# Attention and two expert layers in one kernel: weight blocks loaded and converted later, more warm-up matmuls

## The chip, the cores and the metric

The kernel runs on one core of one Trainium2 chip. The metric is device time in microseconds (us); lower is better. Five engines work side by side, each through its own list of instructions in order: TensorE (PE, matmuls and transposes into PSUM), VectorE (DVE), ScalarE (ACT), GpSimd (POOL) and SyncE (SP), which here does nothing but issue DMA transfers. They wait for each other by semaphores.

## What is computed

All inputs are float32 except `w_in` and `w_out`, which are float64: they reach the kernel as 8-byte words and are turned into float32 on the chip. This turning is what the text calls a conversion.

```
for b in range(12):                      # blocks of 64 positions, per batch (2) and head (8)
    intra = (q_b @ k_b.T * Dmask) @ v_b
    inter = (q_b * lam_pow) @ kv_state
    out[b] = intra + inter
    kv_state = lam**64 * kv_state + (k_b * rev_pow).T @ v_b
...
x = out as 1536 tokens x 512
h = relu(x @ w_in); x = (h * h) @ w_out           # 512 -> 2048 -> 512
...
top-1 routing of x over 8 experts, each 512 -> 1024 -> 512, scaled by two gates
```

## The kernel before, in words

There are three stages. Attention works in 12 units (a batch and a chunk of 128 positions; batches alternate). The dense layer works in steps s (a chunk of 512 tokens and one of 16 slices of `w_in`), and the experts come last. The order of instructions on every engine is the order in which the code is written; nothing reorders them.

One turn u of the attention loop (line 436) writes, in this order: `emit_tmp(u)` on POOL; `wload(WL[u])`, DMA issues for so many weight blocks; `load_qk(u + 4)` and `load_v(u + 3)`, more DMA issues on the same SP queue; `emit_T(u + 2)`, transposes of q and k on PE, five copies on ACT and two products (qd, kd) on POOL; `emit_S(u + 1)`, scores on PE and their mask on DVE (sm); `flush()`, the second half of the conversions that were begun in the turn before; `emit_O(u)`, the output matmuls on PE (L307 with the state, L312 with v), then xTh on ACT and xTl on DVE; `emit_St(u)`, the state's matmuls (L338) and its update on DVE; and `wconv(WA[u], pO)`, the first half of WA[u] conversions. T(u), S(u), O(u), St(u) and sm(u) stand for these pieces below, whatever turn they are written in; q, k and v of unit u are q(u), k(u), v(u).

Weight blocks are numbered i0, i1, ... in the order of loading: even ones are slices of `w_in`, odd ones of `w_out`. A block is 512 KB and lands in one of 4 staging buffers (`st`); the buffer comes free when its conversion is done. q, k and v of one unit are 256 KB each. A conversion (`conv_w`, line 120) has four instructions: ACT scales the high words (L133), DVE shifts the low words (L134), DVE joins the two (L137, `shifted`), and DVE sets the sign (L141, `signed`). Between L133 and L137 the value lies in a PSUM bank, the tile `cv` of pool `pO` with tag "po", of which there is one; with `pool=None` it lies in the destination itself (`wiF`, `woF`) and the joined words in the staging buffer. The last unit's output, `po` of O(11), uses the same single "po" bank.

The weight slices are split once more into a high and a low part for the matmuls (`split_in`: wih on ACT, wil on DVE; `split_out`: woh and wol). `mm1(s)` is 12 matmuls of 512 columns (L367); in each group of three, the first two use wih and the third wil. `mm1(0)` stands in turn 11 ahead of O(11), `mm1(1)` behind the loop, `mm1(2)` in the dense loop behind them. `split_in(0)` and `split_in(1)` stand in turn 10, `split_in(2)` after the activation of step 0. `warm_pe(n)` writes n 128x128 matmuls of the identity into an unused bank.

Of the kernel before, what the change touches and what calls it, by code (L numbers as in the profile page):

```python
# [24 lines left out]
def attn_moe_kernel(ctx, tc, q, k, v, lam, w_in, w_out, w_gate, w_ogate, w1, w2, out):  # L25
# [84 lines left out]
    def load_w(i):  # L110
        f = i // 2
        t = st_p.tile([P, PC], I64, tag="st", name="st")
        if i % 2 == 0:
            nc.sync.dma_start(out=t.rearrange("p (k f) -> p k f", k=KC),
                              in_=w_in[:, f * P:(f + 1) * P].rearrange("(k p) f -> p k f", p=P))
        else:
            nc.sync.dma_start(out=t, in_=w_out[f * P:(f + 1) * P, :])
        staged[i] = t

    def conv_w(i, mid=None):  # L120
        f = i // 2
        t = staged.pop(i)
        if i % 2 == 0:
            dst = wiF[:, :, f * P:(f + 1) * P]
            sh = lambda a: a.rearrange("p (k f) -> p k f", k=KC)
        else:
            dst = woF[:, f, :]
            sh = lambda a: a
        w = t.bitcast(U32).rearrange("p (n w) -> p n w", w=2)
        lo, hi = w[:, :, 0], w[:, :, 1]  # L130
        big = dst if mid is None else sh(mid)
        out_ = sh(lo) if mid is None else big.bitcast(U32)
        nc.scalar.activation(out=big, in_=sh(hi).bitcast(F32), func=AF.Copy, scale=2.0 ** -112)  # L133
        nc.vector.tensor_scalar(out=lo, in0=lo, scalar1=29, scalar2=None, op0=ALU.logical_shift_right)  # L134

        def shifted():
            nc.vector.scalar_tensor_tensor(out=out_, in0=big.bitcast(U32), scalar=3, in1=sh(lo),  # L137
                                           op0=ALU.logical_shift_left, op1=ALU.bitwise_or)

        def signed():  # L140
            nc.vector.scalar_tensor_tensor(out=dst.bitcast(U32), in0=sh(hi), scalar=0x80000000, in1=out_,  # L141
                                           op0=ALU.bitwise_and, op1=ALU.bitwise_or)
        return shifted, signed
# [9 lines left out]
    pO = sa.enter_context(tc.tile_pool(name="pO", bufs=1, space=PSUM))  # L153
# [18 lines left out]
    NU = len(units)  # L172
    qkv = {}

    def load_qk(u):
        b, c = units[u]
        cs = slice(c * P, (c + 1) * P)
        tq = ldqk.tile([P, HP, P], F32, tag="q", name="q")
        for a in range(2):

            nc.sync.dma_start(out=tq[a * D:(a + 1) * D], in_=q[b, a::2, cs, :].rearrange("h (s r) d -> s h (r d)", r=2))
        tk = ldqk.tile([P, H, D], F32, tag="k", name="k")
        nc.sync.dma_start(out=tk, in_=k[b, :, cs, :].rearrange("h s d -> s h d"))
        qkv[u] = [tq, tk]

    def load_v(u):
        b, c = units[u]
        tv = ldv.tile([P, H, D], F32, tag="v", name="v")
        nc.sync.dma_start(out=tv, in_=v[b, :, c * P:(c + 1) * P, :].rearrange("h s d -> s h d"))
        qkv[u].append(tv)  # L190
# [14 lines left out]
    def warm_pe(n):  # L205
        for i in range(n):
            nc.tensor.matmul(out=pw_[:, i % HP, :], lhsT=ident, rhs=ident, start=True, stop=True)
# [43 lines left out]
    def emit_T(u):  # L251
        qt, kt = qkv[u][0:2]
        b, c = units[u]
        psT = pT.tile([P, 2, 2, HP, D], F32, tag="psT", name="psT")
        for hp in range(HP):
            for a in range(2):
                sl = slice(a * D, (a + 1) * D)
                nc.tensor.transpose(psT[:, a, 0, hp, :], qt[sl, hp, :], ident[sl, sl])
        for hp in range(HP):
            for a in range(2):  # L260
                sl = slice(a * D, (a + 1) * D)
                nc.tensor.transpose(psT[:, a, 1, hp, :], kt[sl, 2 * hp:2 * hp + 2, :].rearrange("p h d -> p (h d)"),
                                    ident[sl, sl])
        qT, kT = qT2[u % 2], kT2[u % 2]
        kv = kT.rearrange("p h (g t) -> p g h t", g=2)
        for a in range(2):
            for r in range(2):
                nc.scalar.copy(out=qT[a * D:(a + 1) * D, :, r::2], in_=psT[r * D:(r + 1) * D, a, 0])  # L268
        nc.scalar.copy(out=kv, in_=psT[:, :, 1])
        kTs[u] = kT  # L270
        if c > 0:
            qd = wa.tile([P, HP, P], F32, tag="qd", name="qd")
            nc.gpsimd.tensor_tensor(out=qd, in0=qT, in1=lrow, op=ALU.mult)  # L273
            qds[u] = qd
        if c < NCH - 1:
            kd = wa.tile([P, H, D], F32, tag="kd", name="kd")
            nc.gpsimd.tensor_tensor(out=kd, in0=kt, in1=mask[:, :, P - 1:P].to_broadcast([P, H, D]), op=ALU.mult)  # L277
            kds[u] = kd

    def emit_S(u):  # L280
        qT, kT = qT2[u % 2], kTs.pop(u)
        sm = wa.tile([P, H, P], F32, tag="sm", name="sm")
        ps = [pS.tile([P, HP, P], F32, tag=f"ps{a}", name="ps") for a in range(2)]
        for hp in range(HP):
            for a in range(2):

                sl = slice(a * D, (a + 1) * D)
                nc.tensor.matmul(out=ps[a][:, hp, :], lhsT=kT[sl, hp, :], rhs=qT[sl, hp, :], start=True, stop=True)
        for a in range(2):
            nc.vector.tensor_mul(sm[:, a::2, :], ps[a], mask[:, a::2, :])  # L290
        sms[u] = sm
# [27 lines left out]
    def emit_tmp(u):  # L319
        b, c = units[u]  # L320
        if c in (0, NCH - 1):
            return
        tmps[u] = tmp = wa.tile([P, HP, D], F32, tag="tmp", name="tmp")
        for a in range(2):
            sl = slice(a * D, (a + 1) * D)
            nc.gpsimd.tensor_tensor(out=tmp[sl], in0=state[b][sl, :, a * D:(a + 1) * D], in1=lblk[sl], op=ALU.mult)
# [32 lines left out]
    def mm1(s):  # L359
        ch, f = divmod(s, NF)  # L360
        wih, wil = wis.pop(s)
        ps = pm.tile([P, NTC], F32, tag="ps", name="ps")
        tk = slice(ch * NTC, (ch + 1) * NTC)
        n = 0
        for kk in range(KC):
            for w_, x_ in ((wih, xTh), (wih, xTl), (wil, xTh)):
                nc.tensor.matmul(out=ps, lhsT=w_[:, kk, :], rhs=x_[:, kk, tk], start=n == 0, stop=n == 3 * KC - 1)  # L367
                n += 1
        hps[s] = ps
# [18 lines left out]
    def split_in(s, eng=nc.vector):  # L388
        f = s % NF
        wis[s] = split(wiF[:, :, f * P:(f + 1) * P], "wi", [P, KC, P], eng)  # L390
# [8 lines left out]
    def wload(n):  # L399
        for _ in range(n):  # L400
            if wl[0] < NPC:
                load_w(wl[0])
                wl[0] += 1

    def wconv(n, pool=None):
        m = min(n, NPC - wc[0])
        wc[0] += m
        return [conv_w(wc[0] - m + i, pool and pool.tile([P, PC], F32, tag="po", name="cv")) for i in range(m)]

    rest_ = []  # L410

    def flush():
        for step in range(2):
            for r_ in rest_:
                r_[step]()
        rest_.clear()

    WA = (0,0,0,0,1,1,0,1,1,1,1,1)
    WL = (0,0,1,1,0,1,1,1,1,1,1,1)
    load_qk(2)  # L420
    load_v(0)
    nc.scalar.dma_start(out=tab.rearrange("(p n) w -> p (n w)", p=P), in_=tabi)
# [2 lines left out]
    powers(32, P + 1)  # L425
    for t in state:
        nc.vector.memset(t, 0.0)
    warm_pe(3)
    load_qk(3)
    load_v(1)  # L430
    load_v(2)
# [4 lines left out]
    for u in range(NU):  # L436

        emit_tmp(u)
        wload(WL[u])
        if u + 4 < NU:  # L440
            load_qk(u + 4)
        if u + 3 < NU:
            load_v(u + 3)
        if u + 2 < NU:
            emit_T(u + 2)
        if u == NU - 3:

            sqk.close()
            sp[0] = sab.enter_context(tc.tile_pool(name="sp", bufs=2, side="right", reuse_waits="tile"))
        if u == NU - 2:  # L450
            split_in(0)
        if u < NU - 1:
            emit_S(u + 1)
        if u == NU - 2:
            split_in(1)
        flush()
        if u == NU - 1:
            mm1(0)
        emit_O(u)
        emit_St(u)  # L460
        rest_ += wconv(WA[u], pO)
    flush()
    mm1(1)
    wload(2)
    sa.close()


# [662 lines left out]
```

## Time and profile before

| what | value |
|---|---|
| median of 3 runs | 562.34 us (560.24 to 564.80) |
| profiled execution, its time | 559.54 us |
| profiled execution, its span | 557.7 us |
| PE busy | 537.9 us (96% of the span) |
| DVE busy | 355.5 us (64%) |
| ACT busy | 303.9 us (54%) |
| POOL busy | 151.0 us (27%) |
| granted TensorE clock, mean | 0.994 of full |

Attention fills about the first 58 us of the span, the dense layer the time from there on. The busy shares are means over all stages: which engine or transfer ends the wait is read from the stretch that is asked about. In the timelines a row is a group of like instructions: its start, its length, the engine, the line, what it writes and reads, how many, and in brackets how long the engine had sat idle before it and what ended that.

### The profile page before, as it was taken

The numbers are of one execution on the slowest core, as the hardware profiler recorded it, in microseconds if no ns is written. First come the engines' busy times: TensorE is split into PE (matmuls) and PEld (weight loads), VectorE is DVE, ScalarE is ACT, GpSimd is POOL, SyncE is SP. The second block draws the span as 40 slices with busy tenths as digits, with TensorE's granted clock in tenths as the row PEclk, the third lists the DMA queues.
The fourth block names the chain that finished last, engine by engine and source line by source line (L and its number), as shares of the span: only waits on it lengthen the run. The fifth ranks groups of instructions, "written<-read, shape, count | busy, mean of one in ns | idle before, by whom it ended". The sixth has DMA issues, their size and how long they took to land.

```text
span 557.7 us, 9780 instructions
## 1 busy us (share of the span) xinstructions
PE 537.9 (96%) x3601; PEld 459.3 (82%) x3601; DVE 355.5 (64%) x714; ACT 303.9 (54%) x577; POOL 151.0 (27%) x166
## 2 busy tenths in 40 slices
PE   7998799999999999999999999999999999999994
PEld 6987678877878888887888888889898889888983
DVE  3787788989555674547676446948264949875610
ACT  4766477676643443445445434447264857884610
POOL 8886000000021232422124241450313142240101
PEclk8999999999999999999999999999999999999998
DMA  8999346466500010000000003999738567830000
GB/s 200 235 257 263 117 121 210 164 219 227 193 1 1 20 38 21 1 0 1 19 20 19 20 0 119 368 225 366 216 113 292 194 215 254 285 135 20 9 22 25
DMA packets 75045, 72.88 MB, mean 131 GB/s; under 512 B 30181, under 2 KB 61029, under 8 KB 74976
## 3 DMA queue, kind: packets, MB, share of 16 engines
q1 hardware_dynamic: 70624, 62.96, 36.3%
q0 software_dynamic: 4064, 8.91, 5.1%
q8 instruction: 43, 0.70, 0.5%
q14 instruction: 26, 0.21, 0.1%
q10 hardware_dynamic: 288, 0.10, 0.1%
HBM read 65.84 MB, written 9.29 MB: 135 GB/s over the span
## 4 chain that ended last, share of the span: by engine, by line
PE 71%; issue 12%; DMA 5%; POOL 4%; DVE 3%; ACT 2%; SPq 1%; POOLq 0%; ACTq 0%; DVEq 0%
PE acc L492 23%; PE ps L367 22%; PE ph L931 11%; PE ea L953 10%; DMA k<-in_k_dram 2%; DMA out_dram<-y,sidx 2%; POOL out_dram L963 1%; PE px L705 1%; POOL kd L277 1%; ACT ca L268 1%; PE pt L910 1%; DMA st<-in_moe_w_in_dram 1%; POOL qd L273 1%; PE pl L523 1%; PE po L307 1%
## 5 line engine op out<-in xcount | busy, mean ns | idle before, releaser
L355 POOL TENSOR_TENSOR wol<-woF,woh 128x512 fp32r<-128x512 f32 x32 | 41.4, 1293 | 224.6 <-ACT woh L354 224.6
L385 DVE TENSOR_TENSOR gl<-g,gh 128x512 fp32r<-128x512 f32 x48 | 52.7, 1097 | 65.3 <-ACT gh L384 65.3
L931 PE MATMUL ph<-xh,xTh 128*128 128x192 f32 (+2 forms) x256 | 76.9, 301 | 0.7 <-DVE xl L916 0.5
L367 PE MATMUL ps<-xTh,wih 128*128 128x512 f32 x192 | 76.6, 399 | 0.8 <-ACT wih L354 0.8
L492 PE MATMUL acc<-gl,woh 128*128 128x512 f32 x192 | 75.5, 393 | 0.0
L492 PE MATMUL acc<-gh,woh 128*128 128x512 f32 x192 | 75.0, 390 | 0.5 <-DVE x1T L504 0.5
L367 PE MATMUL ps<-xTh,wil 128*128 128x512 f32 x192 | 74.9, 390 | 0.0
L367 PE MATMUL ps<-xTl,wih 128*128 128x512 f32 x192 | 74.8, 390 | 0.0
L492 PE MATMUL acc<-gh,wol 128*128 128x512 f32 x192 | 74.8, 390 | 0.0
L931 PE MATMUL ph<-xh,xTl 128*128 128x192 f32 (+2 forms) x256 | 74.7, 292 | 0.0
L931 PE MATMUL ph<-xl,xTh 128*128 128x192 f32 (+2 forms) x256 | 74.3, 292 | 0.0
L946 DVE SCALAR_TENSOR_TENSOR hl<-ph,hh 128x384 fp32r<-128x384 f32 (+1 forms) x64 | 34.3, 536 | 61.8 <-ACT hh L945 61.7
L354 ACT CAST woh<-woF 128x512 fp32r<-128x512 f32 x48 | 29.5, 615 | 56.5 <-PE acc L492 56.5
L931 PEld LDWEIGHTS ph<-xh,xTh 128*128 128x128 f32 x256 | 48.6, 190 | 6.9 <-DVE hl L946 4.9
L945 ACT ACTIVATE hh<-ph 128x384 fp32r<-128x384 f32 (+1 forms) x64 | 30.9, 483 | 37.0 <-PE ph L931 33.8
L931 PEld LDWEIGHTS ph<-xl,xTh 128*128 128x128 f32 x256 | 48.6, 190 | 0.8
L931 PEld LDWEIGHTS ph<-xh,xTl 128*128 128x128 f32 x256 | 48.8, 190 | 0.2 <-DVE xTl L806 0.2
L374 ACT ACTIVATE r<-ps 128x512 f32<-128x512 f32 x48 | 28.5, 595 | 35.5 <-PE ps L367 35.5
L890 POOL DMA_INDIRECT xg<-x1d,gidx x21 | 23.9, 1140 | 83.9 <-PE pt L910 62.2
L963 POOL DMA_INDIRECT out_dram<-y,sidx x23 | 23.7, 1030 | 76.9 <-ACT y L962 74.4
L806 DVE TENSOR_TENSOR xTl<-w1r,xTh 128x512 fp32r<-128x512 f32 x64 | 43.7, 686 | 0.1
L492 PEld LDWEIGHTS acc<-gl,woh 128*128 128x128 f32 x192 | 36.1, 188 | 9.1 <-DVE gl L385 1.8
(192 smaller groups left out, 1150.2 us busy)
## 6 DMA issues: line engine op xcount, KB each, us to landing
w1r<-in_moe_w_dram SPq DMA_DIRECT2D x32, 512.0 KB, 6.8
w2r<-in_moe_w_dram SPq DMA_DIRECT2D x32, 512.0 KB, 6.6
st<-in_moe_w_in_dram SPq DMA_DIRECT2D x16, 512.0 KB, 4.3
st<-in_moe_w_out_dram SPq DMA_DIRECT2D x16, 512.0 KB, 3.6
q<-in_q_dram SPq DMA_DIRECT2D x24, 128.0 KB, 3.9
k<-in_k_dram SPq DMA_DIRECT2D x12, 256.0 KB, 4.1
v<-in_v_dram SPq DMA_DIRECT2D x12, 256.0 KB, 4.5
x1d<-xr SPq DMA_DIRECT2D x12, 256.0 KB, 2.0
```

The lines of the kernel that those rows point to most:

```text
L354: nc.scalar.copy(out=hi, in_=src)
L355: eng.tensor_tensor(out=lo, in0=src, in1=hi.bitcast(F32), op=ALU.subtract)
L367: nc.tensor.matmul(out=ps, lhsT=w_[:, kk, :], rhs=x_[:, kk, tk], start=n == 0, stop=n == 3 * KC - 1)
L374: nc.scalar.activation(out=r, in_=ps, func=AF.Relu)
L385: nc.vector.tensor_tensor(out=gl, in0=g, in1=gh.bitcast(F32), op=ALU.subtract)
L492: nc.tensor.matmul(out=acc[ch][cb], lhsT=w_[:, cs], rhs=x_, start=f == 0 and i == 0, stop=f == NF - 1 and i == 2)
L806: eng.tensor_tensor(out=lo, in0=src, in1=hi.bitcast(F32), op=ALU.subtract)
L931: nc.tensor.matmul(out=ps[:, 0:N], lhsT=w_[:, kk, :], rhs=x_[:, kk, 0:N], start=n == 0, stop=n == 3 * KC - 1)
L945: nc.scalar.activation(out=hh[:, f, ts_], in_=ps[:, ts_], func=AF.Relu)
L946: nc.vector.scalar_tensor_tensor(out=hl[:, f, ts_], in0=ps[:, ts_], scalar=0.0, in1=hh[:, f, ts_].bitcast(F32), op0=ALU.max, op1=ALU.subtract)
L953: nc.tensor.matmul(out=ea[j], lhsT=h_[:, f, js], rhs=w_, start=f == 0 and i == 0, stop=f == NF2 - 1 and i == 2)
L963: nc.gpsimd.indirect_dma_start(out=outs[j][:, :], out_offset=bass.IndirectOffsetOnAxis(ap=sidx[:, j, e:e + 1], axis=0), in_=ys[j], in_offs ...
```

## The change

Five lines are edited. The table WL says how many weight blocks a turn loads. Turns 0 to 7 each load q and k of a unit, the last ones in turn 7. Up to and with turn 7, five blocks are loaded in the kernel before (turns 2, 3, 5, 6, 7) and three in the changed one (turns 3, 4, 6); by the end of the loop they are 9 and 8, and the `wload` behind the loop makes it 11 in both. The table WA says how many conversions a turn begins: the same 7, begun in turns 4, 5, 7, 8, 9, 10, 11 before and 5, 6, 8, 9, 10 (two), 11 now. In turns 10 and 11 they no longer use the PSUM bank. The second `warm_pe`, between T(0) and T(1), has 8 calls where it had 3.

```
-    WA = (0,0,0,0,1,1,0,1,1,1,1,1)
-    WL = (0,0,1,1,0,1,1,1,1,1,1,1)
+    WA = (0,0,0,0,0,1,1,0,1,1,2,1)
+    WL = (0,0,0,1,1,0,1,0,1,2,1,1)
...
-    warm_pe(3)
+    warm_pe(8)
...
-        rest_ += wconv(WA[u], pO)
+        rest_ += wconv(WA[u], pO if u < NU - 2 else None)
     flush()
     mm1(1)
-    wload(2)
+    wload(3)
```

SP's queue around the last loads of q and k, before. `q_748` and `k_751` are q(10) and k(10), `q_831` and `k_834` are q(11) and k(11); `st_746`, `st_829`, `st_913` and `st_992` are the blocks i3, i4, i5 and i6.

```order
L117 DMA st_746<-in_moe_w_out_dram 128x512
L181 DMA q_748<-in_q_dram 64x4x128 x2
L183 DMA k_751<-in_k_dram 128x8x64
L189 DMA v_753<-in_v_dram 128x8x64
L114 DMA st_829<-in_moe_w_in_dram 128x4x128
L181 DMA q_831<-in_q_dram 64x4x128 x2
L183 DMA k_834<-in_k_dram 128x8x64
L189 DMA v_836<-in_v_dram 128x8x64
L117 DMA st_913<-in_moe_w_out_dram 128x512
L189 DMA v_915<-in_v_dram 128x8x64
L114 DMA st_992<-in_moe_w_in_dram 128x4x128
```

The blocks i3 and i4 stand ahead of q(11). The same place in the changed kernel, where `q_746`, `k_749` are unit 10, `q_830`, `k_833` unit 11, and `st_744`, `st_911`, `st_988`, `st_990` the blocks i2, i3, i4, i5:

```order
L114 DMA st_744<-in_moe_w_in_dram 128x4x128
L181 DMA q_746<-in_q_dram 64x4x128 x2
L183 DMA k_749<-in_k_dram 128x8x64
L189 DMA v_751<-in_v_dram 128x8x64
L181 DMA q_830<-in_q_dram 64x4x128 x2
L183 DMA k_833<-in_k_dram 128x8x64
L189 DMA v_835<-in_v_dram 128x8x64
L117 DMA st_911<-in_moe_w_out_dram 128x512
L189 DMA v_913<-in_v_dram 128x8x64
L114 DMA st_988<-in_moe_w_in_dram 128x4x128
L117 DMA st_990<-in_moe_w_out_dram 128x512
```

The blocks i3 and i4 have moved behind q(11) and k(11), and i5 follows i4 at once.

DVE's list from the split of wil(1) in turn 10 to the split of wil(2), before; the conversions are those of i4, i5 and i6:

```order
L137 SCALAR_TENSOR_TENSOR cv<-cv,st 128x512
L141 SCALAR_TENSOR_TENSOR wiF<-st,cv 128x4x128
L316 TENSOR_TENSOR xTl<-po,xTh 128x4x128
L134 TENSOR_SCALAR st<-st 128x512
L137 SCALAR_TENSOR_TENSOR cv<-cv,st 128x512
L141 SCALAR_TENSOR_TENSOR woF<-st,cv 128x512
L316 TENSOR_TENSOR xTl<-po,xTh 128x4x128
L134 TENSOR_SCALAR st<-st 128x512
L137 SCALAR_TENSOR_TENSOR cv<-cv,st 128x512
L141 SCALAR_TENSOR_TENSOR wiF<-st,cv 128x4x128
L355 TENSOR_TENSOR wil<-wiF,wih 128x512
```

The first L316 is that of unit 10, the second that of unit 11. The same stretch in the changed kernel, from the last instruction of i3's conversion on (its L137 stands ahead of it), with those of i4 and i5 together and then i6:

```order
L141 SCALAR_TENSOR_TENSOR woF<-st,cv 128x512
L316 TENSOR_TENSOR xTl<-po,xTh 128x4x128
L134 TENSOR_SCALAR st<-st 128x512 x2
L137 SCALAR_TENSOR_TENSOR st<-wiF,st 128x512
L137 SCALAR_TENSOR_TENSOR st<-woF,st 128x512
L141 SCALAR_TENSOR_TENSOR wiF<-st 128x4x128
L141 SCALAR_TENSOR_TENSOR woF<-st 128x512
L316 TENSOR_TENSOR xTl<-po,xTh 128x4x128
L134 TENSOR_SCALAR st<-st 128x512
L137 SCALAR_TENSOR_TENSOR st<-wiF,st 128x512
L141 SCALAR_TENSOR_TENSOR wiF<-st 128x4x128
L355 TENSOR_TENSOR wil<-wiF,wih 128x512
```

There are four conversions in it now, not three, and from L134 x2 on none of them names the PSUM tile `cv`.

## Rows read from the trace of the kernel before

**Rows 1.** The page's chain of waits: shares of the span by engine.
```profile
PE 71%; issue 12%; DMA 5%; POOL 4%; DVE 3%; ACT 2%; SPq 1%; POOLq 0%; ACTq 0%; DVEq 0%
```

**Rows 2.** Stretches: length, busy us (count) by engine, PEclk, DMA share, GB/s.
```profile
40.00:50.00 10.00, 9.39 (x187) 8.63 (x181) 8.03 (x15) 6.80 (x15) 8.53 (x9) 1.00 1.02 266
...
60.00:70.00 10.00, 6.54 (x52) 4.92 (x51) 6.32 (x12) 3.70 (x7) 0.00 (x0) 1.00 0.33 105
```

**Rows 3.** Timeline of PE: start us, us, engine, line, what, [idle before].
```profile
36.31 0.47 PE L258 MATMUL psT<-ident,q 64*128 64x64 f32 x8
37.15 0.46 PE L262 MATMUL psT<-ident,k 64*128 64x64 f32 x8 [0.37 <-DMA k<-in_k_dram]
...
40.85 0.46 PE L258 MATMUL psT<-ident,q 64*128 64x64 f32 x8
...
44.23 0.63 PE L338 MATMUL pt<-v,kd 128*64 128x64 f32 x16
...
51.73 0.46 PE L262 MATMUL psT<-ident,k 64*128 64x64 f32 x8
...
58.42 0.50 PE L367 MATMUL ps<-xTh,wih 128*128 128x512 f32 x1
```

**Rows 4.** Timeline of PE: O(11), and the first and third matmul of mm1(2).
```profile
64.09 1.09 PE L307 MATMUL po<-qd,ca 128*64 128x128 f32 x16 [2.61 <-DVE woF L141]
...
69.88 0.50 PE L367 MATMUL ps<-xTh,wih 128*128 128x512 f32 x1 [0.84 <-ACT wih L354]
...
70.61 0.50 PE L367 MATMUL ps<-xTh,wil 128*128 128x512 f32 x1
```

**Rows 5.** Timeline of DVE, from sm(10) to wil(2).
```profile
53.17 1.29 DVE L290 TENSOR_TENSOR sm<-ps,ca 128x512 f32<-128x512 f32 x2 [1.08 <-PE ps L288]
...
57.55 0.68 DVE L355 TENSOR_TENSOR wil<-wiF,wih 128x512 fp32r<-128x512 f32 x1
...
60.79 0.69 DVE L141 SCALAR_TENSOR_TENSOR wiF<-st,cv 128x512 uint32<-128x512 uint32 x1
...
66.71 0.69 DVE L316 TENSOR_TENSOR xTl<-po,xTh 128x512 fp32r<-128x512 f32 x1 [2.77 <-ACT xTh L315]
...
68.11 0.70 DVE L137 SCALAR_TENSOR_TENSOR cv<-cv,st 128x512 uint32<-128x512 uint32 x1 [0.38 <-ACT cv L133]
...
69.86 0.69 DVE L355 TENSOR_TENSOR wil<-wiF,wih 128x512 fp32r<-128x512 f32 x1 [0.33 <-ACT wih L354]
```

**Rows 6.** The chain of waits in order of time: start us, us, what; k(10) and i6.
```profile
41.35 4.79 DMA k<-in_k_dram
...
51.78 4.29 DMA st<-in_moe_w_in_dram
```

**Rows 7.** Stretches up to the landing of k(7), k(8), k(11): GB/s stand last.
```profile
0.00:32.57 32.57, 27.91 (x448) 25.73 (x448) 18.49 (x38) 19.88 (x43) 27.33 (x57) 0.95 0.89 222
0.00:37.15 37.15, 32.07 (x528) 29.57 (x529) 22.37 (x44) 23.06 (x50) 30.61 (x60) 0.95 0.90 226
...
0.00:51.73 51.73, 44.93 (x768) 41.28 (x769) 34.77 (x68) 32.68 (x70) 42.69 (x73) 0.97 0.92 233
```

**Rows 8.** Groups on DVE by form, 0 to 200 us: conversions without and with PSUM.
```profile
L137 DVE SCALAR_TENSOR_TENSOR st<-wiF,st 128x512 uint32<-128x512 uint32 x12 | 8.2, 686 | 0.0
...
L137 DVE SCALAR_TENSOR_TENSOR cv<-cv,st 128x512 uint32<-128x512 uint32 x7 | 4.9, 693 | 0.5 <-ACT cv L133 0.4
```

**Rows 9.** Timeline of POOL: qd(10).
```profile
48.80 1.28 POOL L273 TENSOR_TENSOR qd<-ca,ca 128x512 f32<-128x512 f32 x1 [1.21 <-PE po L307]
```

**Rows 10.** Timeline of PE, early: second warm-up, T(1).
```profile
6.75 0.94 PE L207 MATMUL pw__157<-ident 128*128 128x128 f32 x6
9.14 0.69 PE L258 MATMUL psT<-ident,q 64*128 64x64 f32 x8 [1.46 <-ACT ca L269]
```

**Rows 11.** Stretches around two waits of PE; PEclk is third from the end.
```profile
9.00:12.00 3.00, 2.86 (x32) 2.64 (x32) 0.00 (x0) 1.69 (x6) 2.96 (x5) 0.50 0.94 226
...
61.00:64.00 3.00, 0.47 (x3) 0.04 (x1) 2.80 (x5) 0.64 (x1) 0.00 (x0) 1.00 0.39 118
```

## The prediction

> **What bounds the kernel now.** The page's chain of waits comes first: 71% of the span is PE work, so time is saved where PE waits [rows 1]. The view by stretches shows where that is: between 60 and 70 us PE works 6.54 of 10 us, at the seam between attention and the dense layer [rows 2]. Over the whole span PE is busy for 96%, so I take what follows the seam as fixed: the kernel ends earlier by what the third matmul of mm1(2) starts earlier, now at 70.61 [rows 4]. (It is the third because the first two need only wih.)
>
> Two waits set that moment. PE's timeline at the seam shows O(11) waiting 2.61 us for the last instruction of i5's conversion, an L141 on DVE, because O(11) and the conversions share one PSUM bank [rows 4]. Ahead of the seam PE waits for q and k: in the stretch from 40 to 50 us the DMA engines are at 1.02 of their time, at 266 GB/s [rows 2], and T(11) gets k at 51.73 [rows 3]. T(9) at 40.85 began without a wait, 44.23 + 0.63 = 44.86 is the end of St(7), and from the end of T(11) to mm1(0) at 58.42 PE works on end [rows 3].
>
> **Loads.** Two blocks leave the queue ahead of k(11): 2 x 0.524 MB at 266 GB/s is 3.9 us, so k(11) can land at 51.73 - 3.9 = 47.8 [rows 2, 3]. Ahead of k(8) stand i0 and i1 in both kernels, so I leave its landing at 37.15 at first [rows 3]. From there PE alone sets the pace. A turn of PE costs 44.86 - 40.85 = 4.0 us, so T(10) can start at 44.86 and T(11) at 48.9, where k(11) has landed [rows 3]. T(11)'s q part and k part take 0.55 us together at the pace of T(9) (40.85 to S(8) at 41.40), so its k part starts at 49.2. The way from there to mm1(0) stays 58.42 - 51.73 = 6.7 us: **mm1(0) at 55.9, 2.5 us earlier** [rows 3]. POOL allows it: its wait of 1.21 us ahead of qd(10) was for O(8), so qd(10) can come at 47.6, and O(10), which reads it, would come at about 54 [rows 9].
>
> The cover that goes: i3, i4 and i5 are now loaded behind k(11). From 47.8 on, v(10), i3, v(11), i4 and i5 are 2.1 MB, or 7.9 us at 266 GB/s: i5 lands at 55.7 [rows 2]. The new SP list issues i6 when i2's conversion has freed its buffer, about 53, and it would land near 58.
>
> **Conversions.** DVE goes from the start of wil(0) at 57.55 to that of wil(2) at 69.86 in 12.31 us, of which it waits 2.77 + 0.38 + 0.33 = 3.48: 8.8 us of work for three conversions [rows 5]. The change puts a fourth in. By their mean its L137 and L141 take 2 x 686 ns = 1.4 us [rows 8]. Its short L134 I set against what alternation gives back: of i4 and i5 each L137 and L141 no longer waits for the result of the one just before it. So 10.2 us. Writing to SBUF instead of PSUM changes nothing on DVE: 686 against 693 ns [rows 8].
>
> When does wil(0) start? sm(10) came at 53.17 after a wait of 1.08 [rows 5]. PE would allow 2.5 us less, 50.7, but DVE is now busy with unit 8's xTl, state and i2's L134 until about 50.8, so sm(10) moves by 2.4 and wil(0) to 55.2. Then wil(2) starts at 65.4, and the third matmul follows 70.61 - 69.86 = 0.75 later, as now: **66.2** [rows 4, 5].
>
> PE would be ready before that. O(11) needs the bank of i3's conversion, which stands where i4's does now: that ends at 60.79 + 0.69 = 61.48, 3.9 us after wil(0) starts [rows 5], so at 59.1, just as mm1(0) is done (55.9 and 12 matmuls, 3.1 us). O(11) takes 1.9, mm1(1) 3.1, and the third matmul follows 0.73 after the first [rows 4]: 64.8. So the 2.61 us wait disappears, and **a new wait of about 1.4 us on DVE's wil(2) takes part of its place**. ACT is not late: xTh(11), i6, r, g and wih(2) are five operations of about 0.6 us behind O(11)'s end at 61.0, done at 64.1. wload(3) has i8, i9 and i10 wait for buffers that come free from 62.5 on; they are needed after the seam, so they cost nothing as long as they land within the 5 us until the dense loop reaches them.
>
> **Warm-up.** Three calls make six rows and 0.94 us; eight take 2.5 us, from 6.75 to 9.26, and T(1) stood at 9.14 behind 1.46 us of idling [rows 10]: 0.1 us later. After that idling the granted clock was 0.50, the lower level of 1.2 GHz, from 9 to 12 us [rows 11]. Kept at 2.4 GHz, T(1) and S(0) could be about 1 us shorter. I price both ends at nothing: T(8) waits for k(8) anyway. If that cover went, the warm-up would be worth up to 0.7 us.
>
> **The sum.** 70.61 - 66.2 = 4.4 us. What stays unknown is k(8). By 37.15 the chip had moved 226 x 37.15 = 8.40 MB; ahead of k(8)'s end in SP's list stand 7.7 MB (18 loads of q and k for nine units, v of seven, two blocks, a small table). For k(7) the same surplus is 7.23 - 6.92 = 0.3 MB, for k(11) 12.05 - 11.63 = 0.4 MB [rows 7]. Before, v(7) and i2 stood right behind k(8) and were in flight with it; now i2 does not. So k(8) lands between 37.15 and (8.40 - 0.3) MB / 226 GB/s = 35.9, and everything behind it moves along: 0 to 1.2 us. I take 0.4, nearer to its own row than to the other two. **4.8 us, 0.85%.** The profiled execution took 559.54, 2.8 under the median; against the median of 562.34 the forecast is 557.5.
>
> The Trainium skill (DMA: Bandwidth & Descriptors, on two DMAs through one engine) says that the transfers of one queue start in order but are pipelined. By order alone k(8) would land at 35.9, and the sum would be 5.6; the surplus at k(8) speaks for the pipelining.
>
> **Rivals.**
> - *The loads do not come earlier* (what is moved aside does not hold q and k up). For it: k(8) shows that landing is not a matter of order alone [rows 7]. Against it: the full DMA engines [rows 2] and the 4.79 us that k(10) took from issue to landing [rows 6]. Then only the bank counts: wil(0) stays at 57.55, wil(2) at 67.75, the third matmul at 68.5: 2.1 us, 560.2. Chance 0.10.
> - *The clock falls in attention.* k(7) has one block less ahead, k(8) does not, so PE's waits gather at T(8): St(5), which ends at 36.31 now, can be done near 34.7, while k(8) comes at 37.15 [rows 3]. Idling of 1.46 us stood once ahead of 3 us at 0.50 [rows 10, 11]; 2.61 us at the seam, behind 512-column matmuls, left the clock at 1.00 [rows 11]. 3 us at half rate lose 1.5: 559.0. Chance 0.12. The Trainium skill (TensorE: Matmul & The Clock Gate, on HAM oscillation) tells of a kernel whose DMA waits between bursts threw it to the lower clock; the early rows here agree, the seam's do not.
> - *q and k come earlier still*, k(8) at 35.9 or POOL freed by the warm-up too: 5.6 to 6.2 us, 556.5. Chance 0.15.
> - *The blocks come too late, slower.* i4 and i5 are converted one turn after they are loaded, where i4 had two. DVE reaches the L134 of i5 at 55.2 + 4.8 = 60.0; the landing is due at 55.7. Every us past 60.0 moves wil(2) and all behind it; past 64.8 the kernel is slower than before, and at 70 us it takes 567.5. For it: the chain already shows a block, i6, that took 4.29 us to land [rows 6]. Against it: 4 us of slack, and free DMA engines after 60 us (0.33) [rows 2]. Chance 0.05.
>
> **How the numbers follow.** The forecast has 0.58, the rivals 0.10, 0.12, 0.15 and 0.05. The range takes in the first three rivals, 1.2 us for k(8), and about 1 us for a median whose runs spread from 560.24 to 564.80: 554.9 to 560.9. A measurement of this kernel tells about 1%, or 5.6 us, from no change. The forecast lies under that bound; I give a third of it to more than 5.6 (0.19), and most of the earlier-still case (0.11) and a trace of the others: faster 0.31, same 0.63, slower 0.06.
>
> **What would show it.** T(11) waits for no DMA and starts near 48.9; mm1(0) near 55.9; O(11) has no wait of over 0.3 us; the third matmul of mm1(2) waits over 1 us for wil(2), at about 66; the granted clock stays 1.00 from 9 to 12 us. A third matmul after 68, a T(11) that still waits for k, or a clock of 0.50 near 37 us would make it wrong.

## The result, and the profile after

| kernel | median us | lowest to highest | runs |
|---|---|---|---|
| before | 562.32 | 560.24 to 564.80 | 6 |
| changed | 556.74 | 555.17 to 557.80 | 6 |

The ratio is 0.9895, with a 95% interval of 0.9865 to 0.9925: 5.6 to 5.9 us faster. The profiled execution of the changed kernel took 557.8 us, the slowest of its six, with a span of 556.0 us.

The page's chain of waits has more PE in it than [rows 1], 77% for 71%:

```profile
PE 77%; issue 9%; DVE 5%; DMA 4%; POOL 2%; ACT 1%; POOLq 0%; SPq 0%; DVEq 0%; ACTq 0%
```

The same stretches as [rows 2] and [rows 11], and two single microseconds (the columns are those of [rows 2]):

```profile
9.00:12.00 3.00, 1.67 (x33) 1.47 (x32) 1.17 (x2) 2.10 (x6) 2.96 (x5) 1.00 0.95 230
40.00:50.00 10.00, 8.39 (x152) 7.77 (x150) 8.11 (x15) 6.07 (x13) 7.21 (x8) 0.91 0.87 220
...
45.00:46.00 1.00, 0.00 (x0) 0.01 (x1) 1.00 (x2) 0.00 (x0) 1.00 (x2) 1.00 0.32 74
46.00:47.00 1.00, 0.59 (x10) 0.48 (x10) 0.97 (x3) 0.00 (x0) 0.93 (x2) 1.00 0.18 49
...
60.00:70.00 10.00, 8.24 (x58) 6.06 (x57) 9.83 (x18) 5.82 (x11) 0.00 (x0) 1.00 0.51 171
```

At the seam (last row) PE works 8.24 of 10 us where it had 6.54, and DVE 9.83 where it had 6.32. Ahead of it, from 40 to 50 us, the DMA engines are *less* busy than before, 0.87 for 1.02, with two microseconds in which they almost stand still, and PE with them in the first (0.00) and for part of the second (0.59). PE's timeline, with the pieces of [rows 3, 4]:

```profile
36.52 0.46 PE L258 MATMUL psT<-ident,q 64*128 64x64 f32 x7 [1.16 <-DMA q<-in_q_dram]
37.08 0.47 PE L262 MATMUL psT<-ident,k 64*128 64x64 f32 x8
...
46.02 0.55 PE L258 MATMUL psT<-ident,q 64*128 64x64 f32 x8 [1.22 <-DMA q<-in_q_dram]
46.96 0.46 PE L262 MATMUL psT<-ident,k 64*128 64x64 f32 x8 [0.39 <-DMA k<-in_k_dram]
47.26 1.18 PE L288 MATMUL ps<-ca,ca 64*128 64x128 f32 x16
48.37 1.97 PE L307 MATMUL po<-qd,ca 128*64 128x128 f32 x16
50.13 1.76 PE L312 MATMUL po<-sm,v 128*64 128x128 f32 x16
...
52.58 0.41 PE L262 MATMUL psT<-ident,k 64*128 64x64 f32 x8
...
59.21 0.50 PE L367 MATMUL ps<-xTh,wih 128*128 128x512 f32 x1
...
62.97 1.09 PE L307 MATMUL po<-qd,ca 128*64 128x128 f32 x16 [0.76 <-DVE woF L141]
...
67.91 0.50 PE L367 MATMUL ps<-xTh,wih 128*128 128x512 f32 x1
...
69.63 0.50 PE L367 MATMUL ps<-xTh,wil 128*128 128x512 f32 x1 [0.98 <-DVE wil L355]
```

T(8) and T(10) still wait for q and k. O(8) at 48.37 takes 1.97 and 1.76 us where others take 1.09 and 1.04: the granted clock was 0.50, the lower level of 1.2 GHz, from 48.17 to 51.58. So T(11)'s k part begins at 52.58 and mm1(0) at 59.21, both 0.8 us *later* than in the profile before. T(11) no longer waits there, but k(11) was not earlier: it was issued at 46.69 and landed 5.1 us later, at 51.8. Only then comes the gain: O(11) waits 0.76 us for the bank where it waited 2.61, and the third matmul of mm1(2) starts at 69.63, 0.98 earlier. There PE waits for wil(2), as DVE's timeline shows, which runs on end:

```profile
58.89 0.69 DVE L355 TENSOR_TENSOR wil<-wiF,wih 128x512 fp32r<-128x512 f32 x1
...
62.14 0.69 DVE L141 SCALAR_TENSOR_TENSOR woF<-st,cv 128x512 uint32<-128x512 uint32 x1
...
63.34 0.76 DVE L134 TENSOR_SCALAR st<-st 128x512 uint32<-128x512 uint32 x2
...
68.89 0.68 DVE L355 TENSOR_TENSOR wil<-wiF,wih 128x512 fp32r<-128x512 f32 x1
```

From wil(0) to wil(2) it takes 10.0 us for four conversions; before it took 12.31 for three, with 3.48 of waiting [rows 5].

The warm-up rows answer to [rows 10]; the clock from 9 to 12 us is 1.00 (stretches above) where it was 0.50 (what that rests on: e5 below):

```profile
6.75 2.25 PE L207 MATMUL pw__157<-ident 128*128 128x128 f32 x16
9.14 0.47 PE L258 MATMUL psT<-ident,q 64*128 64x64 f32 x8
```

The two profiled executions differ by 1.7 us of span, the medians by 5.6. So the profiles must be compared with more executions, which the experiments gave.

### The profile page after: what moved, and what is told of

The parts are those of the page before. It is cut to its first block, busy times and chain, and to the rows that moved or that the text cites. A ratio compares the mean times of both kernels' runs of the same rounds, so it can differ in the third digit from the quotient of the medians.

```text
span 556.0 us, 9798 instructions
## 1 busy us (share of the span) xinstructions
PE 538.4 (97%) x3611; PEld 461.4 (83%) x3611; DVE 354.8 (64%) x714; ACT 303.4 (55%) x577; POOL 150.6 (27%) x166
## 4 chain that ended last, share of the span: by engine, by line
PE 77%; issue 9%; DVE 5%; DMA 4%; POOL 2%; ACT 1%; POOLq 0%; SPq 0%; DVEq 0%; ACTq 0%
PE acc L492 23%; PE ps L367 22%; PE ph L931 13%; PE ea L953 11%; DMA k<-in_k_dram 3%; PE po L307 1%; POOL out_dram L963 1%; PE px L705 1%; PE pt L910 1%; PE ps L288 1%; DMA out_dram<-y,sidx 1%; PE pw__157 L207 1%; PE po L312 1%; PE pl L523 1%; ACT ca L268 1%
## 5 line engine op out<-in xcount | busy, mean ns | idle before, releaser
L492 PE MATMUL acc<-gh,woh 128*128 128x512 f32 x192 | 74.9, 390 | 0.5 <-DVE x1T L504 0.5
L492 PE MATMUL acc<-gl,woh 128*128 128x512 f32 x192 | 74.9, 390 | 0.0
L492 PE MATMUL acc<-gh,wol 128*128 128x512 f32 x192 | 74.7, 389 | 0.0
L367 PEld LDWEIGHTS ps<-xTh,wil 128*128 128x128 f32 x192 | 36.0, 188 | 9.1 <-DVE wil L355 1.4
```

The source lines that it names most:

```text
L492: nc.tensor.matmul(out=acc[ch][cb], lhsT=w_[:, cs], rhs=x_, start=f == 0 and i == 0, stop=f == NF - 1 and i == 2)
```

## The experiments

All were timed in five rounds beside the kernel before on the same chip (its medians there: 562.25 to 563.05). Each profile is one execution. The table puts them side by side, in us: blocks loaded ahead of k(11); the start of T(11)'s k part; from there to the third matmul of mm1(2); from there to the first L492 matmul of step 12 (the second matmul of the dense layer, `mm2(12)`). What follows that point takes 418.2 to 419.7 us in all fourteen profiles.

| kernel | median (ratio, 95%) | blocks | T(11) k | to third | to mm2(12) | mm2(12) at |
|---|---|---|---|---|---|---|
| before | 562.32 | 5 | 51.73 | 18.88 | 68.47 | 139.08 |
| e4 before, again | 563.23 (0.9999, 0.9971 to 1.0027) | 5 | 53.96 | 20.05 | 68.44 | 142.45 |
| e5 warm-up alone | 563.48 (1.0006, 0.9979 to 1.0033) | 5 | 53.57 | 20.41 | 68.46 | 142.44 |
| e6 seam filled | 562.47 (0.9992, 0.9968 to 1.0016) | 5 | 54.42 | 18.90 | 68.50 | 141.82 |
| e1 bank alone | 559.25 (0.9934, 0.9911 to 0.9956) | 5 | 55.67 | 15.76 | 68.28 | 139.71 |
| e2 changed, loads as before | 558.69 (0.9931, 0.9904 to 0.9958) | 5 | 53.94 | 16.56 | 67.73 | 138.23 |
| changed | 556.74 (0.9895, 0.9865 to 0.9925) | 3 | 52.58 | 17.05 | 67.73 | 137.36 |
| e3 changed, again | 557.30 (0.9901, 0.9873 to 0.9929) | 3 | 53.33 | 16.56 | 67.72 | 137.61 |
| e9 ACT's order | 556.35 (0.9882, 0.9864 to 0.9900) | 3 | 51.58 | 16.55 | 67.70 | 135.83 |
| e12 e9, blocks by ACT | 556.61 (0.9879, 0.9850 to 0.9908) | 3 | 51.51 | 16.66 | 67.69 | 135.86 |
| e8 i6 later | 559.18 (0.9934, 0.9906 to 0.9961) | 3 | 51.88 | 15.11 | 71.29 | 138.28 |
| e10 i6 later, ACT's order | 556.81 (0.9888, 0.9870 to 0.9906) | 3 | 52.16 | 15.11 | 69.30 | 136.57 |
| e11 e10, two blocks ahead | 557.87 (0.9903, 0.9880 to 0.9926) | 2 | 51.65 | 16.25 | 69.29 | 137.19 |
| e7 no blocks ahead | 560.11 (0.9946, 0.9924 to 0.9968) | 0 | 46.43 | 23.13 | 69.29 | 138.85 |

### e1: the bank alone

```
 (kernel before)
-        rest_ += wconv(WA[u], pO)
+        rest_ += wconv(WA[u], pO if u < NU - 2 else None)
```

> The kernel before with one edit: the conversions begun in turns 10 and 11 (i5 and i6) leave the PSUM bank. If the bank alone carries the gain, this is as fast as the whole change, about 556.7 us. If the later loads carry a part, it gains less. By DVE's list: wil(0) stays at 57.55, its 8.8 us of work follow without the 3.5 us of waiting, wil(2) starts near 66.4 and the third matmul of mm1(2) near 67.1, 3.5 us earlier than before: 558.8; about 0.7 us more if the dense loop starts with more slack, 558.1.

Measured: 559.25 us, 3.8 less than before and a little over the 558.1 to 558.8 expected. The two waits that answer to [rows 4]:

```profile
65.59 1.09 PE L307 MATMUL po<-qd,ca 128*64 128x128 f32 x16 [0.22 <-DVE wiF L141]
...
71.43 0.50 PE L367 MATMUL ps<-xTh,wil 128*128 128x512 f32 x1 [0.17 <-DVE wil L355]
```

The bank was worth 2.4 us of waiting, and from T(11) to the third matmul 15.76 us where the four profiles with the bank have 18.88 to 20.41. This one line is about two thirds of the whole gain.

### e2 and e3: the changed kernel with the loads of before, and unchanged

```
 (changed kernel; e2)
-    WL = (0,0,0,1,1,0,1,0,1,2,1,1)
+    WL = (0,0,1,1,0,1,1,1,1,1,1,1)
...
-    wload(3)
+    wload(2)
```

> The changed kernel with the load table of the kernel before (five blocks ahead of the last q and k, wload(2) behind the loop); conversions, bank and warm-up as changed. If the later loads bring q and k forward, T(11) gets k near 51.7 again, wil(0) starts near 57.5, four conversions make wil(2) 67.6 and the third matmul 68.3: 2.3 us to 3.0 us under before, 559.3 to 560.0, so 2.6 to 3.3 us slower than the whole change. If the loads are worth nothing, it stays at 556.7.

> The changed kernel, unedited, for a second profile. Its six runs spread from 555.2 to 557.8 us, and the profiled one was the slowest. If the half-rate stretch at 48 to 52 us in that profile cost 1.7 us and is not in every execution, a profile of a run near 555.5 has the clock at 1.00 through attention and the third matmul of mm1(2) near 67 to 68 us. If it belongs to the change, it is there again, with T(10) waiting over 1 us.

Measured: 558.69 and 557.30 on the same chip: the later loads are worth 1.4 us by the medians, with intervals of the ratios that overlap; e2 lies between its two expectations. T(11) came at 53.94 with five blocks ahead and at 53.33 with three. In e3 a stretch at 0.50 came again, but in another place: from 39.5 to 43.0 us, behind a wait of T(8) of 1.24 us for q.

### e4 and e5: the kernel before again, and the warm-up alone

e4 has no edit. e5:

```
 (kernel before)
-    warm_pe(3)
+    warm_pe(8)
```

> The kernel before, unedited, for a second profile beside the one that all the prediction rests on. If the stall structure is fixed, the third matmul of mm1(2) is again within 0.5 us of 70.6 and O(11) waits 2.6 us for the bank. If landings of q and k vary between executions, T(11) gets k at another time, and runs spread by 2 to 4 us (560.2 to 564.8 so far).

> The kernel before with eight warm-up calls for three, nothing else. If the early gain is absorbed where the unit loop waits for k, the time stays at that of the kernel before, 563 us, with the clock at 1.00 from 9 to 12 us. If warm-up shifts everything behind it, it gains up to 0.7 us. A third way: it only moves the half-rate stretch to a later place, and then it gains nothing or loses up to 1.7 us.

Measured: 563.23 and 563.48. With eight calls T(1) starts at 8.73 and the clock is 1.00 from 9 to 12 us, where e4 has 0.50; but T(8) gets k at 37.65 where e4 has 37.59: nothing is left of it. Nor is it shown that the eight calls keep the clock up. All ten profiles with eight calls have 1.00 there, but so have e1 and e6, which have three calls and the same 1.46 us of idling ahead of T(1) as the two profiles of the kernel before. The stretch of e1:

```profile
9.00:12.00 3.00, 1.62 (x34) 1.43 (x34) 1.29 (x2) 2.13 (x5) 2.96 (x5) 1.00 0.91 220
```

In e4 T(11) came at 53.96 and the third matmul at 74.01, both over 2 us later than in the profile that the prediction was read from. O(11) waited 2.66 us, as in [rows 4]; here the clock fell to 0.50 behind it, from 66.93 to 70.34.

### e6: PE kept busy while O(11) waits

```
 (kernel before, behind mm1(0))
+            pf = pO.tile([P, HP, P], F32, tag="pt", name="pf")
+            for i in range(8):
+                nc.tensor.matmul(out=pf[:, i % HP, :], lhsT=ident, rhs=ident, start=True, stop=True)
```

> The kernel before with eight more 128x128 matmuls into an idle PSUM bank between mm1(0) and O(11), 2.3 us of PE work inside the wait of 2.6 us for the bank; the wait itself stays. If the wait of O(11) costs only its own length, nothing changes: 563 us. If the idling at the seam throws the clock to half rate in some executions (in the second profile of the kernel before it was 0.50 from 66.9 to 70.3 us), the median falls by about 1 us and the slowest runs, 565 to 567 us, go.

Measured: 562.47, not to be told from before. The clock stayed at 1.00 at the seam, and T(11) to the third matmul took 18.90 where e4 and e5, with the fall, took 20.05 and 20.41. One execution of three with that seam and no filling (the first profile) had no fall either, and took 18.88. So the fall takes about 1.2 to 1.5 us where it comes, by these four executions, and too little over all runs to be measured: none of e6's twelve runs came to 565 us, where 6 of the 33 beside it did, too few to tell.

### e7: no block ahead of the last q and k

```
 (changed kernel)
-    WA = (0,0,0,0,0,1,1,0,1,1,2,1)
-    WL = (0,0,0,1,1,0,1,0,1,2,1,1)
+    WA = (0,0,0,0,0,0,0,0,3,1,2,1)
+    WL = (0,0,0,0,0,0,0,0,3,2,1,1)
...
-        rest_ += wconv(WA[u], pO if u < NU - 2 else None)
+        rest_ += wconv(WA[u], None)
...
-    wload(3)
+    wload(4)
```

> The changed kernel with no weight block ahead of the last q and k: three in turn 8, two in turn 9, one each in turns 10 and 11, four behind the loop; all conversions from turn 8 on and without the bank. It is a probe for the landing of k(11), not meant to be fast: seven conversions, 12 us of DVE work, now follow turn 8. If landing goes by the bytes ahead, k(11) lands three blocks, 5 to 6 us, earlier than in the changed kernel (52.6 and 53.3 us there), and PE's pace of 4.0 us a turn is the limit, T(11) near 48. If the issuing of q, k and v on SP is the limit, k(11) lands within 2 us of where it landed with three blocks ahead.

Measured: no turn from T(6) on waits for q or k; each takes 3.95 us, and T(11)'s k part begins at 46.43. So k(11) had landed over 5 us earlier than with three blocks, and the issuing of q, k and v alone is not the limit. But 23.13 us pass from there to the third matmul, since the conversions all stand behind it, and ACT, whose copies S(11) needs, now waits for their blocks (1.65 us ahead of its L133 at 48.01):

```profile
53.46 2.05 PE L288 MATMUL ps<-ca,ca 64*128 64x128 f32 x16 [3.31 <-ACT ca L269]
...
59.56 0.50 PE L367 MATMUL ps<-xTh,wil 128*128 128x512 f32 x1 [0.78 <-DVE wil L355]
```

With no block ahead the wait for q and k is gone, but the time is given back at the conversions: 560.11 us, over 3 us above the changed kernel.

### e8, e9, e10: is the dense loop bound by the conversions?

PE waits for wil(2), which stands behind i6's conversion on DVE. e8 moves that conversion behind the attention loop; the added lines stand in the first step of the dense loop, behind split_out(0):

```
 (changed kernel; e8)
-    WA = (0,0,0,0,0,1,1,0,1,1,2,1)
+    WA = (0,0,0,0,0,1,1,0,1,1,2,0)
...
+            rest_ += wconv(1)
+            flush()
```

> The changed kernel with the conversion of i6 moved from turn 11 to behind split_out(0), still ahead of split_in(3), which needs it. wil(2) then comes about 1.8 us earlier on DVE and no longer holds PE: the third matmul follows the first of mm1(2) by 0.7 us and not 1.7. If what follows the seam is fixed, the kernel gains 1.0 us: 555.9 to 556.3. If DVE's total work until the last conversion (at about 148 us) is the limit, as the loss of pace behind 100 us in the first profile suggests, it gains 0.2 us or less.

Measured: the third matmul came at 66.99, 2.6 us earlier than in the changed profile, and the loop took 3.6 us more to mm2(12): more lost than won, and a time of 559.18, which neither expectation had. DVE's steps in that loop, and ACT's instructions that they wait for:

```profile
87.62 0.68 DVE L385 TENSOR_TENSOR gl<-g,gh 128x512 fp32r<-128x512 f32 x1
...
89.57 0.69 DVE L355 TENSOR_TENSOR wol<-woF,woh 128x512 fp32r<-128x512 f32 x1 [0.59 <-ACT woh L354]
...
93.19 0.68 DVE L385 TENSOR_TENSOR gl<-g,gh 128x512 fp32r<-128x512 f32 x1
```

```profile
88.39 0.64 ACT L377 ACTIVATE g<-r 128x512 f32<-128x512 f32 x1 [0.55 <-DVE gl L385]
88.93 0.60 ACT L354 CAST woh<-woF 128x512 fp32r<-128x512 f32 x1
```

It is a ring: ACT's g waits for DVE's gl of the step before (there is one buffer for g), ACT's woh stands behind g, DVE's wol waits for woh, and the next gl stands behind wol. A step takes 93.19 - 87.62 = 5.57 us, where a PE that does not wait takes 10.88 us for two. e9 opens the ring in the changed kernel, e10 in e8:

```
 (e9: changed kernel, act1; e10: the same in e8)
         r = gp[0].tile([P, NTC], F32, tag="r", name="r", bufs=1)
         nc.scalar.activation(out=r, in_=ps, func=AF.Relu)
         g = gp[0].tile([P, NTC], F32, tag="g", name="g", bufs=1)
+        if mid is not None and 0 < s < NF - 1:
+            mid()
+            mid = None
```

> The changed kernel, with ACT's order in the dense loop altered: woh and wih of the next steps are written ahead of g of the same step, so they no longer stand behind g's wait for DVE's gl. Theory (the first conversion steps are paced by a ring of DVE gl, ACT g, ACT woh, DVE wol at 5.57 us a step, PE alone would take 5.44): the ring opens, but in the changed kernel PE is short of its own pace by only about 0.2 us up to 160 us, so 0 to 0.5 us is won: 556.3 to 557.3. Rival (order of ACT is not the limit, and g later holds up the second matmul): 1 us or more slower, over 558. The seam does not move: mm1(0) and the third matmul of mm1(2) as in the changed kernel, within what executions differ (67 to 70 us).

> i6's conversion moved behind the loop as in e8, and ACT's order as in e9. Theory: e8 won 2.6 us at the seam and lost it in the dense loop because DVE and ACT were held in their ring with one conversion more to do; with the ring open the first 144 matmuls of the second kind take near 65.5 us, as in the changed kernel, not 69.0. The third matmul of mm1(2) near 67.0, the 144th near 135, time 554 to 555.5. Rival (the sum of DVE's work up to 140 us is the limit, whatever the order): the loop still takes over 68 us, 558 to 559.5, and all that is won ahead of the loop by moving conversions behind the seam is an advance on work that DVE has to do anyway.

Measured: 556.35 and 556.81. In e10 DVE's step is shorter, 96.20 - 91.09 = 5.11, and no row of these waits:

```profile
91.09 0.69 DVE L388 TENSOR_TENSOR gl<-g,gh 128x512 fp32r<-128x512 f32 x1
...
92.58 0.69 DVE L355 TENSOR_TENSOR wol<-woF,woh 128x512 fp32r<-128x512 f32 x1
...
96.20 0.69 DVE L388 TENSOR_TENSOR gl<-g,gh 128x512 fp32r<-128x512 f32 x1
```

The first matmul of mm2(0) to that of mm2(12) took 66.96 us in e10, 68.99 in e8, 65.34 in the changed kernel: the theory's 65.5 and the rival's 68 both missed. Of the 3.6 us that e8 lost, the ring is 2.0. The other 1.6 lies around one wait of PE, 0.99 us for gl at 76.83 in e10, and that gl stands behind i6's conversion on DVE; that DVE has this work to do in either place is argued from its order, not tried. e9 gained 0.4 and 0.95 us against the two medians of the changed kernel, about what was expected and too little to be told from it; from the third matmul to mm2(12) its profile has 67.70 us for 67.73.

### e11 and e12: what holds k(11) up?

```
 (e10; e11)
-    WL = (0,0,0,1,1,0,1,0,1,2,1,1)
+    WL = (0,0,0,0,1,0,1,0,2,2,1,1)
```

> As e10, with two weight blocks, not three, loaded ahead of the last q and k. Theory of the prediction (DMA engines full, so each block ahead costs its 2 us): k(11) 2 us earlier than in e10. Theory after the first runs (landing of q and k is set by when SP's issue instructions get through, with stalls of 3.4 us, and only an empty queue removes the wait): 0 to 1 us earlier, T(11) still waits for k, near 51 us; time within 0.7 us of e10.

```
 (e9, load_w; e12)
+        eng = nc.scalar if i < 3 else nc.sync
...
-            nc.sync.dma_start(out=t, in_=w_out[f * P:(f + 1) * P, :])
+            eng.dma_start(out=t, in_=w_out[f * P:(f + 1) * P, :])
```

> As e9, with the three weight blocks ahead of the last q and k issued by ACT instead of SP, so that SP's list up to k(11) holds q, k and v alone, in the number of bytes that e9 moves too. Theory A (the DMA engines' throughput sets when q and k land): no change, T(11) still waits for k at 51.5 to 53. Theory B (SP gets q and k out too late, because its issue instructions for q stall up to 4 us behind the blocks): SP's issues of q take under 2.6 us each, as with no blocks ahead; k(11) lands 2 us or more earlier, T(11) at 47 to 49.5 and 0 to 2 us less time than e9's 556.35. ACT issues three blocks at 0.4 to 1.3 us each, which it can spare in the turns where PE waits; a slower time would come from there.

Measured in e11: T(11)'s k part at 51.65 with two blocks ahead, 0.5 us before e10's, and a time of 557.87, 1.1 above e10, with intervals that overlap. T(11) did not wait for k: k(11), issued at 45.82, landed 5.4 us later, at 51.2, where e10's, issued at 47.02, landed 5.1 us later, at 52.1. That is 0.9 us for one block, not the 2 us of a full DMA. What held T(10), and with it T(11), was ACT, which waited for the block i1, and then the clock, 0.50 to 0.56 from 46 to 49.5 us:

```profile
43.00 0.65 ACT L133 ACTIVATE cv<-st 128x512 f32<-128x512 f32 x1 [3.47 <-DMA st<-in_moe_w_out_dram]
```

```profile
45.84 0.56 PE L258 MATMUL psT<-ident,q 64*128 64x64 f32 x8 [2.54 <-ACT ca L269]
```

So loading one block later was paid for here by that block's coming too late for its conversion, as in the last rival of the prediction.

SP's own timeline shows why k(11) gained so little. In the kernel before (rows are DMA issues; the second number is how long the issuing took):

```profile
45.23 1.26 SPq L181 DMA_DIRECT2D q<-in_q_dram  x2
46.59 0.55 SPq L183 DMA_DIRECT2D k<-in_k_dram  x1
```

in the changed kernel:

```profile
39.14 1.34 SPq L181 DMA_DIRECT2D q<-in_q_dram  x2
40.58 0.55 SPq L183 DMA_DIRECT2D k<-in_k_dram  x1
41.23 1.28 SPq L189 DMA_DIRECT2D v<-in_v_dram  x1
42.56 4.03 SPq L181 DMA_DIRECT2D q<-in_q_dram  x2
46.69 0.55 SPq L183 DMA_DIRECT2D k<-in_k_dram  x1
```

and in e12, where no block stands in SP's list ahead of these:

```profile
41.03 5.71 SPq L182 DMA_DIRECT2D q<-in_q_dram  x2
46.84 0.55 SPq L184 DMA_DIRECT2D k<-in_k_dram  x1
```

The stretches of e12 in which it ends:

```profile
45.00:46.00 1.00, 0.83 (x18) 0.60 (x14) 0.97 (x3) 0.45 (x1) 1.00 (x2) 1.00 0.26 51
46.00:47.00 1.00, 0.00 (x0) 0.00 (x0) 1.00 (x2) 0.00 (x0) 1.00 (x2) 1.00 0.14 33
```

In the changed kernel SP reaches q(11) at 42.56, 2.7 us earlier than before, where the two issues took 1.26 us from 45.23 on. But now they take 4.03 us, and in the last two of these the DMA engines run dry (0.32 and 0.18 above); k(11) is issued at 46.69, and was at 46.59. In e11 SP gets there at 40.17 and stays 5.55 us, to 45.72. In e12 theory A has its number (T(11) at 51.51) but not its reason: the engines were at 0.94 to 1.25 of their time in each microsecond from 41 to 45, and then at 0.26 and 0.14. Theory B has the stall, but not the blocks as its cause.

In the changed kernel, e9, e10, e11 and e12 the stall ends at 46.59, 46.13, 46.92, 45.72 and 46.74, each time 0.2 to 0.3 us before k(10) lands (46.9, 46.4, 47.3, 45.9 and 47.1, by its issue and its time to landing). The buffer is not what SP waits for: q(11) takes that of q(7), which PE had read by 31.3 us in the changed kernel. What holds SP there was not found.

## Why the prediction came out as it did

The forecast was 557.5, the median is 556.74, and 4.8 us were forecast where 5.6 came. The terms do not add up as they were put, and that the total came within 0.8 us is in part luck: the loads gave 0.6 less than their term and k(8) 0.4 less, the conversions 1.0 more, and what was taken as fixed 0.7 more. Two of the prediction's own signs of being wrong came: the third matmul after 68 us (69.63), and a T(11) that still waits for k (0.57 us in e3).

**Conversions: right, and the larger part.** 10.2 us of DVE work from wil(0) to wil(2) were reckoned, 10.0 measured. The bank's wait goes (0.76 and, in e3 and e9, 0.20 left), the new wait for wil(2) was put at 1.4 us and is 0.98. From T(11)'s k part to the third matmul 66.2 - 49.2 = 17.0 us were forecast, 16.55 to 17.05 measured in five profiles (e2, changed, e3, e9, e12); before, in four, 18.88 to 20.41. The term was 1.9 and is 2.9 between the medians of these groups (19.5 and 16.6), because the profile that the prediction was read from was the shortest of the four; the two longest are those in which the clock fell at the seam.

**Loads: the step that failed.** "Two blocks leave the queue ahead of k(11): 2 x 0.524 MB at 266 GB/s is 3.9 us, so k(11) can land at 51.73 - 3.9 = 47.8"; and from there PE was to set the pace, with T(11) at 48.9 and no wait for DMA. T(11) still waits in five of the six profiles with three blocks ahead; in e9:

```profile
51.58 0.46 PE L262 MATMUL psT<-ident,k 64*128 64x64 f32 x8 [0.97 <-DMA k<-in_k_dram]
```

Over the six profiles with five blocks ahead T(11)'s k part begins at 51.73 to 55.67, median 53.95; over the six with three, at 51.51 to 53.33, median 52.0: 1.9 us, where 2.5 were in the sum and 3.9 were to be had. The step takes a full DMA for given; SP's early arrival at q(11) turned into a longer issue and idle DMA engines. And the landing of one execution was taken for the kernel's: 51.73 is the earliest of those six, by 1.8 us. The profile after, with k(11) landing at 51.8, seemed to refute the loads altogether.

**Assumed fixed: what follows the seam.** It gave another 0.7 us, 67.7 for 68.5 from the third matmul to mm2(12), by the ring of e8. DVE's step of 5.57 us loses 0.13 to PE's 5.44. In the kernel before, gl of step 1 starts 1.44 us ahead of the matmul that reads it, and from 111.42 us on PE is held for about 0.1 us in each step; in the changed kernel it starts 2.14 us ahead, and PE is held first at 137.60. With 1.9 and 2.9 that is 5.5, near the measured 5.6. e1 to e3 divide it by medians: 3.8 for the bank, 0.6 for the order of conversions with the warm-up (not told from nothing), 1.4 for the loads.

**Warm-up: right to be priced at nothing.** T(8)'s wait absorbs it, and e5 shows no gain by itself. The clock is 1.00 from 9 to 12 us, but e1 and e6 have that without the added calls, so the reason that was given for it is not shown.

**k(8):** 0.4 us were taken; T(8)'s k part came at 37.08 for 37.15, and nothing of it was seen.

**Rivals.** *The clock falls in attention*: it did, behind T(10) and not behind T(8) in the profile after, and behind T(8) in e3, as the rival had it. In the profile after T(10) to T(11) took 5.6 us where a turn takes 4.0; but k(11) landed only at 51.8, so T(11) was 0.8 us later by it, not 1.5. It is a matter of the execution: the clock fell in attention in e1, e3, e7 and e11 too, but not in e2, e8, e9, e10 and e12. The Trainium skill (TensorE: Matmul & The Clock Gate, on HAM oscillation) has DMA waits between bursts as the cause of such falls. These runs agree that the falls come behind waits (2.26 us for q in e1, 3.31 for ACT in e7), and differ in that it doesn't happen every time: 1.82 us for k in e2 left the clock at 1.00. *The loads do not come earlier* was half true in its mechanism and not in its time, since the bank alone gave more than the 2.1 us it was priced at. *Blocks too late*: not in the changed kernel, where no conversion up to the seam waited for a block and DVE ran on end from 52.55 us; in e7 and e11, which load them later still, ACT did wait for blocks. *Earlier still* did not come.

## What to carry to other kernels

Before pricing a wait that ends with a DMA landing, get several executions: with five blocks ahead T(11) got its k at times that differ by up to 4 us, the distance from there to the seam differed by 1.5, and the forecast was read from one execution of both. Bytes taken out of a queue are worth their transfer time only as long as the issuing engine keeps the queue full; look at the issuing engine's own rows, not only at the DMA share. When a saving ahead of a loop vanishes in it, look for a ring of engines in it whose step is close to the loop's own.

## What was not expected of the hardware

- SP's two issues of one q took 1.26 us, or up to 5.71, and in the last two microseconds of such a stall the DMA engines were at 0.14 to 0.32 of their time (changed kernel, e12); moving the weight blocks to ACT's queue did not change that.
- Whole stretches at the lower clock came and went between executions of the same instructions: in e4 from 66.93 to 70.34 behind a wait of 2.66 us at the seam, in the first profile of the same kernel, behind 2.61 us, not. From 9 to 12 us, behind the same 1.46 us of idling, the clock was 0.50 in the two profiles of the kernel before and 1.00 in e1 and e6.
